# First four token chunks on different PSUM tiles, weight and activation loads on other queues, and the second tile's cast and transposes one step earlier

## The chip, the cores and the metric

The kernel runs on one core of one Trainium2 chip. A core has four compute engines that run side by side, each with its own queue of instructions: TensorE (PE in the profile, its weight loads PEld), VectorE (DVE), ScalarE (ACT) and GpSimd (POOL). SyncE (SP) issues data transfers (DMAs). An engine takes its instructions in the order in which they were written, and an instruction that waits holds back everything behind it on that engine. The metric is the device time of one execution in microseconds (us), smaller is better.

## What is computed

The input x has 8 sequences of 4096 tokens with 192 channels. A causal convolution of 7 taps mixes each token with the six before it; the 24 channels of each of 8 heads share one set of tap weights, a softmax over 7 numbers. The result goes through a two-layer network with 2048 hidden units and the activation h * sigmoid(beta * h). Cut to what matters:

```python
w = softmax(weight, axis=-1)                         # 8 heads x 7 taps
out = np.einsum('hk,bskhg->bshg', w, x_unf)          # x_unf: the 7 last tokens of each token
h = out.reshape(32768, 192) @ w_in                   # 192 -> 2048
g = h * (1.0 / (1.0 + np.exp(-beta * h)))
return (g @ w_out).astype(np.float32)                # 2048 -> 192
```

## The kernel before

**Tiling.** The 32768 tokens are two streams of 16384 (s = 0 and 1) that are worked side by side, each on 64 of the 128 partitions; the 192 channels are three groups (kk) of 64. A *tile* j is 512 tokens of both streams. The work goes in *steps* (lines 65 to 69): steps 0 and 1 take 128 tokens of each stream, step 2 takes 256, steps 3 to 8 take 256 each, and all later ones take 512. In step i the kernel runs the first matmul (mm1) of step i, with the activation on ScalarE right behind it, and between its units the second matmul (mm2) of step i-1. A step has 16 units of 128 hidden columns; steps 0 to 2 take them in pairs (`mm1_pair`, u = 0 to 7: hidden columns u and u + 8, one on each half of the partitions, so that only half of w_in is needed on each), later steps one by one (`mm1`, u = 0 to 15).

**The order of the work** is written out by hand: `pin` keeps every instruction in program order on its engine. Waits between engines are derived from the tiles that instructions read and write.

**Start (lines 116 to 252).** The tap weights, the first chunk of x and beta are loaded by SP and ACT. GpSimd builds the two masks `sel` and `ident` and then issues its loads: four pieces of w_in, chunks 1 to 3 of x (`load_x0`, 128 tokens of both streams each), four pieces of w_out, four pieces of the second tile of x (`load_x(1, ...)`), then four copies of w_in from one half of the partitions to the other, and at last the casts of blocks 2 and 3 of the second tile. The softmax of the taps is left unnormalised in `etap`; its sum's reciprocal `rsum` is applied on the way out of PSUM. Seven diagonal matrices `diag[k]` hold the taps. `warm` issues matmuls on zeros, whose result nobody reads.

**The first tile (chunks b = 0 to 3)** is convolved on TensorE: `transpose_0` (three transposes into PSUM), `take_0` (copy to `xr`), `halo_0` (last six columns to the next chunk), `conv_0` (14 matmuls with `diag`), `evac_0` (scaled copy to `xc_of`, one for each stream). Chunk 0 is done before step 0, chunks 1 to 3 between the units of step 0 and after u = 0 of step 1. `scale_w_out` (VectorE, 16 pieces) divides w_out by beta between them.

**PSUM** is two pools of two tiles, each of two banks: `psum_h` (name ph) and `psum_o` (name po). A tile that is asked for waits until the one that had the buffer two requests earlier is no longer in use. Before the change one `misc` tile of psum_h holds the output of `warm`, the taps and beta, and `cv0`, the other psum_h tile, holds both streams of chunk 0's convolution.

**From the second tile on** (step 3 and later) the convolution is VectorE's: `cast_x` (float32 to bfloat16), `transpose_x` (DMA transpose on SP, one per block of 128 tokens) into `xt`, then `conv_ops`: tap 0 on line 279, taps 1 to 6 on line 281, the last one writing `xc`, which mm1 reads. `load_x` fetches tiles two ahead on SP. These operations stand in the list `work`, and `vector_work` writes them out between the units of mm1: each call adds to a budget (1300 in step 2, 653 in steps 3 to 8), and operations are written while the budget is above zero, each costing its planned ns (929 for a 256-token tap, 850 for a cast). Since DVE runs in program order, this decides also how much work stands ahead of `store` (line 356), the copy of a finished mm2 result out of psum_o.

**Step 2, u = 0, before the change** casts blocks 0 and 1 of the second tile, issues its four transposes and the loads of tile 3; at the end of step 1 the loads of tile 2 have been issued. `vector_work` begins at u = 1.

Of the kernel before, what the change touches and what calls it, by code (L numbers as in the profile page):

```python
# [10 lines left out]
FP32 = mybir.dt.float32  # L11
# [8 lines left out]
def kernel(  # L20
# [60 lines left out]
    def cast_x(j, s, b0=0, b1=NB, eng=None):  # L81
        if j not in xbf_of:
            xbf_of[j] = xbf_pool.tile([128, NB, NK, NS, Q], BF16, name="xb")
        pin((eng or nc.vector).tensor_copy(  # L84
            xbf_of[j][:, b0:b1, :, s, :].rearrange("p b k q -> p k b q"),
            xf_of[j][:, b0:b1, s, :].rearrange("p b (q k) -> p k b q", k=NK)))
# [4 lines left out]
    def transpose_x(j, b):  # L91
        if j not in xt_of:
            new_xt(j)
        c = LEAD + 128 * b
        pin(nc.sync.dma_start_transpose(  # L95
            out=xt_of[j][:, :, c:c + 128],
            in_=xbf_of[j][:, b, :, :, :].rearrange("p k s q -> p (k s q)")))
# [30 lines left out]
    scrap = consts.tile([128, 1], FP32, name="scrap")  # L128
    pin(nc.scalar.activation(scrap, one, AF.Exp))


    sel = consts.tile([H, NS, H, Q // H], FP32, name="sel")
    pin(nc.gpsimd.memset(sel, 0.0))
# [3 lines left out]
    pin(nc.gpsimd.memset(ident, 0.0))  # L137
    pin(nc.gpsimd.affine_select(out=ident, in_=ident, compare_op=ALU.not_equal, fill=1.0,
                                base=0, pattern=[[-1, 128]], channel_multiplier=1))
    HF = F // 2  # L140

    def load_x0(b):
        pin(nc.gpsimd.dma_start(out=x0[:, b, :, :],
                                in_=xs[:, 128 * b:128 * b + 128, :].rearrange("s p d -> p s d")))

    for f in range(0, HF, 512):
        for s in range(NS):
            load_w_in(s, HF * s + f, HF * s + f + 512)
        if f == 0:
            load_x0(1)  # L150
    load_x0(2)
    for c in range(0, NF, 4):
        pin(nc.gpsimd.dma_start(out=w_out_f[:, c:c + 4, :], in_=w_out_v[:, c:c + 4, :]))
        if c == 0:
            load_x0(3)
    for b in (0, 2):
        for s in range(NS):
            load_x(1, s, b, b + 2, nc.gpsimd)
# [3 lines left out]
    for s in range(NS):  # L162
# [5 lines left out]
    ident2 = consts.tile([128, NS, Q], FP32, name="ident2")  # L168
    pin(nc.vector.tensor_tensor(out=ident2, in0=ident[:, None, 0:Q].to_broadcast([128, NS, Q]),
                                in1=ident[:, None, Q:].to_broadcast([128, NS, Q]), op=ALU.add))  # L170
    misc = psum_h.tile([128, 2, TILE], FP32, name="ph")

    def warm(n, cols):
        for _ in range(n):
            pin(nc.tensor.matmul(misc[:, 0, 0:cols], zeros[:, 0:128], zeros[:, 0:cols], start=True, stop=True))  # L175

    warm(9, 256)
    tap_ps = misc[:, 1, 0:K]
    pin(nc.tensor.matmul(tap_ps, sel.rearrange("h s g j -> h (s g j)"), taps, start=True, stop=True))
    nmax = consts.tile([128, 1], FP32, name="nmax")  # L180
    pin(nc.vector.tensor_reduce(out=nmax, in_=tap_ps, axis=AX.X, op=ALU.max, negate=True))
# [1 line left out]
    tsum = consts.tile([128, 1], FP32, name="tsum")  # L183
    pin(nc.scalar.activation(etap, tap_ps, AF.Exp, bias=nmax, accum_out=tsum))
    diag = consts.tile([128, K, NS, Q], FP32R, name="diag")
    for k in range(K):
        pin(nc.vector.tensor_scalar_mul(diag[:, k, :, :], ident2, etap[:, k:k + 1]))
    rsum = consts.tile([128, 1], FP32, name="rsum")
    pin(nc.vector.reciprocal(rsum, tsum))


    place = [(0, 0), (1, 0), (2, 0), (2, 128)]
# [21 lines left out]
    def conv_0(cv, b, k0=0, k1=K):  # L214
        for k in range(k0, k1):
            for s in range(NS):
                pin(nc.tensor.matmul(  # L217
                    cv[:, s, 0:NK * 128], diag[half_of(s), k, :, :].rearrange("p s q -> p (s q)"),
                    xr[b][half_of(s), :, k:k + 128], start=(k == 0), stop=(k == K - 1)))

    def evac_0(cv, b, s, eng):
        i, c = place[b]
        src = cv[:, s, 0:NK * 128].rearrange("p (k t) -> p k t", k=NK)
        dst = xc_of[i][:, s, :, c:c + 128]
        if eng is nc.scalar:
            pin(nc.scalar.activation(dst, src, AF.Copy, scale=rsum))
        else:
            pin(eng.tensor_scalar_mul(dst, src, rsum))  # L228

    def po_tile():  # L230
        return psum_o.tile([128, 2, TILE], FP32, name="po")

    new_xt(0)
    po01 = po_tile()
    t0_ = transpose_0(po01[:, 0, :], 0)
    take_0(t0_, 0, act=True)
    beta_ps = misc[:, 1, 16:16 + NF]
    pin(nc.tensor.transpose(beta_ps, beta16, ident[0:NF, 0:NF]))
    beta = consts.tile([128, NF], FP32, name="beta")
    pin(nc.vector.tensor_copy(beta, beta_ps))  # L240
    warm(3, 128)
    pin(nc.scalar.activation(scrap, one, AF.Silu))
    cv0 = psum_h.tile([128, 2, TILE], FP32, name="ph")
    conv_0(cv0, 0)
    evac_0(cv0, 0, 0, nc.scalar)
    evac_0(cv0, 0, 1, nc.vector)
    warm(6, 128)
    rbeta = consts.tile([128, NF], FP32, name="rbeta")
    pin(nc.vector.reciprocal(rbeta, beta))
    tapn = consts.tile([128, K], FP32, name="tapn")  # L250
# [89 lines left out]
    def mm2(i, pr, phase, fc):  # L340
        if phase == 0 and fc == 0:
            po_of[pr] = psum_o.tile([128, 2, TILE], FP32, name="po")
        po = po_of[pr]
        for half in range(2):
            q = half ^ phase
            s, b = pr[q]
            r = half_of(half)
            pin(nc.tensor.matmul(po[:, q, 0:D], g_of[i][r, fc, s, ts(b, 128)], w_out_s[r, fc, :],  # L348
                                 start=(phase == 0 and fc == 0), stop=(phase == 1 and fc == NF - 1)))
        if phase == 1 and fc == NF - 1:  # L350
            store(i, pr, po)
# [56 lines left out]
    for i in range(n_steps):  # L408
        plan = mm2_plan(i - 1) if i else [[] for _ in range(NF)]
        g_of[i] = g_pool.tile([128, NF, NS, TILE], BF16, name="g")  # L410
        if i == 0:
            for u in range(NF // 2):
                mm1_pair(0, u)
                if u == 0:
                    t = transpose_0(po01[:, 1, :], 1)
                    take_0(t, 1)
                    halo_0(t, 1)
                elif u == 1:
                    cv = po_tile()
                    conv_0(cv, 1)  # L420
                    for s in range(NS):
                        evac_0(cv, 1, s, nc.vector)
                elif u == 2:
                    po23 = po_tile()
                    t = transpose_0(po23[:, 0, :], 2)
                    take_0(t, 2)
                    halo_0(t, 2)
                elif u == 4:
                    cv = po_tile()
                    conv_0(cv, 2)  # L430
                    for s in range(NS):
                        evac_0(cv, 2, s, nc.vector)
                elif u == 6:
                    t = transpose_0(po23[:, 1, :], 3)
                    take_0(t, 3)
                    halo_0(t, 3)
                if u >= 4:
                    for c in range(2 * (u - 4), 2 * (u - 3)):
                        scale_w_out(c)
            continue  # L440
        if i < NP:
            for u in range(NF // 2):
                mm1_pair(i, u)
                if i == 1 and u == 0:
                    for c in range(8, 12):
                        scale_w_out(c)
                    cv = po_tile()
                    conv_0(cv, 3)
                    for c in range(12, NF):
                        scale_w_out(c)  # L450
                    for s in range(NS):
                        evac_0(cv, 3, s, nc.vector)
                for t in plan[2 * u] + plan[2 * u + 1]:
                    mm2(i - 1, *t)
                if i == 2:
                    if u == 0:
                        for s in range(NS):
                            cast_x(1, s, 0, 2)
                        for b in range(NB):
                            transpose_x(1, b)  # L460
                        for s in range(NS):
                            load_x(3, s)
                    else:
                        vector_work(i, 1300, flush=u == NF // 2 - 1)
            if i == 1:
                for s in range(NS):
                    load_x(2, s)
            continue
        for u in range(NF):
            mm1(i, u)  # L470
            for t in plan[u]:
# [34 lines left out]
```

## Time and profile before

| | |
|---|---|
| median of 3 runs | 703.62 us (702.87 to 704.54) |
| the profiled execution: its own time / its span from first to last instruction | 704.65 us / 702.9 us |
| TensorE busy (matmuls / weight loads) | 689.8 / 542.6 us |
| VectorE, ScalarE, GpSimd busy | 541.4, 587.4, 15.9 us |
| PE busy in 0 to 50 us | 39.9 of 50 us |
| PE busy in 50 to 690 us | 640 of 640 us |
| DMA, share of 16 engines' time, 11 to 18 us | 1.01 to 1.08 |

The row of PE in 0 to 50 us is the sum of five stretches of 10 us (7.45, 9.43, 8.74, 7.40, 6.91). Between 50 and 690 us the matmuls follow each other without a gap. The profile counts a matmul as busy over its whole length though neighbours overlap, so a busy PE is not a measure of throughput. Numbers such as L348 are lines of the kernel; x16 behind a row means 16 instructions merged.

### The profile page before, as it was taken

What the parts mean: (1) busy time and instruction counts of PE and PEld (TensorE: products, weight loads), DVE (VectorE), ACT (ScalarE), POOL (GpSimd) and SP (SyncE); (2) the same over time, 40 slices, a digit from 0 to 9 for tenths busy, and PEclk for the clock granted to TensorE, in tenths of its full rate; (3) what the DMA queues carried; (4) which work ended last, traced back from release to release, by engine and by line L of the source; (5) the groups of instructions that cost most, each with busy time, mean ns of one, the idle gap of its engine ahead of it and who ended that gap; (6) DMA issues with size and microseconds to landing.
All of it is one profiled execution on the core that took longest, in us unless ns stands there. A gap on an engine that the chain in (4) does not pass through costs nothing.

```text
span 702.9 us, 25421 instructions
## 1 busy us (share of the span) xinstructions
PE 689.8 (98%) x11561; PEld 542.6 (77%) x11561; DVE 541.4 (77%) x901; ACT 587.4 (84%) x600; POOL 15.9 (2%) x29
## 2 busy tenths in 40 slices
PE   8879999999999999999999999999999999999998
PEld 5669997777777777777777777777777777777777
DVE  3499999999988877877977787887787887785002
ACT  4869999888888888888888888888888888888882
POOL 7100000000000000000000000000000000000000
PEclk9999999999999999999999999999999999999999
DMA  8535333434433342334342333343333342111112
GB/s 207 132 92 159 103 104 92 117 109 109 112 103 101 105 114 64 89 104 100 104 114 77 80 101 97 104 114 80 82 97 103 97 114 70 48 47 47 33 40 69
DMA packets 120572, 67.33 MB, mean 96 GB/s; under 512 B 55024, under 2 KB 119616, under 8 KB 120464
## 3 DMA queue, kind: packets, MB, share of 16 engines
q1 hardware_dynamic: 118336, 61.08, 31.6%
q0 software_dynamic: 1984, 4.52, 2.8%
q8 instruction: 90, 1.47, 0.9%
q14 instruction: 18, 0.15, 0.1%
q10 hardware_dynamic: 144, 0.10, 0.1%
HBM read 28.32 MB, written 25.17 MB: 76 GB/s over the span
## 4 chain that ended last, share of the span: by engine, by line
PE 94%; DMA 2%; DVE 2%; POOL 1%; SPq 0%; issue 0%; ACT 0%; POOLq 0%; DVEq 0%
PE po L348 46%; PE ph L311 46%; PE po L371 2%; DMA w_in_s<-in_moe_w_in_dram 1%; DMA xf<-in_x_dram 1%; DVE acc L281 1%; DMA xt<-xb 0%; PE ph L298 0%; POOL w_in_s L110 0%; PE po L217 0%; POOL xf L78 0%; DVE w_out_s L255 0%; SPq L95 0%; DVE xc L281 0%; SPq L78 0%
## 5 line engine op out<-in xcount | busy, mean ns | idle before, releaser
L314 ACT ACTIVATE g<-ph,beta 128x1024 bf16<-128x1024 f32 (+1 forms) x544 | 561.0, 1039 | 89.7 <-PE ph L311 86.0
L348 PEld LDWEIGHTS <-g 64*128 64x128 bf16 x7936 | 362.3, 94 | 92.8 <-issue 0.2
L348 PE MATMUL po<-w_out_s,g 64*128 64x192 bf16 x7936 | 427.9, 243 | 0.0
L311 PE MATMUL ph<-xc,w_in_s 64*128 64x512 bf16 (+1 forms) x3264 | 420.3, 358 | 5.0 <-DVE xc L281 5.0
L281 DVE SCALAR_TENSOR_TENSOR acc<-xt,tapn,acc 128x512 f32<-128x512 bf16 (+1 forms) x450 | 315.3, 763 | 0.9
L311 PEld LDWEIGHTS <-w_in_s 64*128 64x128 bf16 x3264 | 168.9, 94 | 51.6 <-issue 5.2
L356 DVE COPY o_sb<-po 128x384 f32<-128x384 f32 x124 | 69.0, 557 | 130.6 <-PE po L348 128.8
L281 DVE SCALAR_TENSOR_TENSOR xc<-xt,tapn,acc 128x512 bf16<-128x512 bf16 (+1 forms) x90 | 64.2, 763 | 0.2
L84 DVE CAST xb<-xf 128x768 bf16<-128x768 f32 (+1 forms) x62 | 48.9, 826 | 0.0
L279 DVE TENSOR_SCALAR acc<-xt,tapn 128x512 f32<-128x512 bf16 (+1 forms) x90 | 40.5, 501 | 6.5 <-DMA xt<-xb 5.4
L302 ACT ACTIVATE g<-ph,beta 128x256 bf16<-128x256 f32 (+1 forms) x48 | 22.0, 564 | 7.4 <-PE ph L298 6.9
L298 PE MATMUL ph<-xcp,w_in_s 64*128 64x256 bf16 (+1 forms) x144 | 15.2, 320 | 2.1 <-ACT g L302 1.4
L298 PEld LDWEIGHTS <-w_in_s 64*128 64x128 bf16 x144 | 7.2, 98 | 6.2 <-issue 4.2
L371 PE MATMUL po<-w_out_s,g 128*128 128x192 bf16 x128 | 10.7, 246 | 0.0
L371 PEld LDWEIGHTS <-g 128*128 128x128 bf16 x128 | 10.5, 98 | 0.2 <-issue 0.2
L374 DVE COPY o_sb<-po 128x192 f32<-128x192 f32 x8 | 2.9, 358 | 7.6 <-PE po L371 7.6
L228 DVE TENSOR_SCALAR xcp<-po,rsum 128x384 bf16<-128x384 f32 x6 | 3.4, 610 | 4.2 <-PE po L217 4.2
L217 PE MATMUL po<-xr,diag 64*128 64x384 f32 x42 | 5.7, 415 | 0.6 <-DVE xr L208 0.6
L175 PE MATMUL ph<-zeros 128*128 128x256 bf16 (+1 forms) x18 | 3.4, 362 | 2.4 <-DVE beta L240 1.3
L217 PEld LDWEIGHTS po<-xr,diag 64*128 64x128 f32 x42 | 4.5, 230 | 1.3 <-DVE xr L208 1.2
L175 PEld LDWEIGHTS <-zeros 128*128 128x128 bf16 x18 | 2.1, 137 | 3.3 <-issue 1.8
L270 DVE COPY xt<-xt 128x18 bf16<-128x18 bf16 x28 | 4.5, 160 | 0.0
(46 smaller groups left out, 42.9 us busy)
## 6 DMA issues: line engine op xcount, KB each, us to landing
out_dram<-o_sb SPq DMA_DIRECT2D x124, 192.0 KB, 2.7
xf<-in_x_dram SPq DMA_DIRECT2D x60, 384.0 KB, 4.2
xt<-xb SPq DMA_TRANSPOSE x124, 2.4
w_out_f<-in_moe_w_out_dram POOLq DMA_DIRECT2D x4, 384.0 KB, 7.5
w_in_s<-in_moe_w_in_dram POOLq DMA_DIRECT2D x4, 192.0 KB, 6.1
xf<-in_x_dram POOLq DMA_DIRECT2D x4, 192.0 KB, 7.3
w_in_s<-w_in_s POOLq DMA_DIRECT2D x4, 192.0 KB, 7.5
out_dram<-o_sb SPq DMA_DIRECT2D x8, 96.0 KB, 1.6
```

Source lines behind the costliest of these rows:

```text
L84: pin((eng or nc.vector).tensor_copy(xbf_of[j][:, b0:b1, :, s, :].rearrange("p b k q -> p k b q"), xf_of[j][:, b0:b1, s, :].rearrange("p b ...
L175: pin(nc.tensor.matmul(misc[:, 0, 0:cols], zeros[:, 0:128], zeros[:, 0:cols], start=True, stop=True))
L217: pin(nc.tensor.matmul(cv[:, s, 0:NK * 128], diag[half_of(s), k, :, :].rearrange("p s q -> p (s q)"), xr[b][half_of(s), :, k:k + 128], sta ...
L279: pin(nc.vector.tensor_scalar_mul(a, src, w))
L281: pin(nc.vector.scalar_tensor_tensor(out=xc_of[i][:, k0:k1, 0:n] if k == K - 1 else a, in0=src, scalar=w, in1=a, op0=ALU.mult, op1=ALU.add))
L298: pin(nc.tensor.matmul(ph[:, h, 0:NS * n], w_in_s[half_of(h), kk, ts(fcs[h], 128)], xc_of[i][half_of(h), :, kk, :], start=(kk == 0), stop= ...
L302: pin(nc.scalar.activation(g_of[i][:, fcs[h], :, 0:n], ph[:, h, 0:NS * n].rearrange("p (s t) -> p s t", s=NS), AF.Silu, scale=beta[:, fcs[ ...
L311: pin(nc.tensor.matmul(ph[:, s, 0:n], w_in_s[half_of(s), kk, ts(fc, 128)], xc_of[i][half_of(s), kk, 0:n], start=(kk == 0), stop=(kk == NK ...
L314: pin(nc.scalar.activation(g_of[i][:, fc, :, 0:n], ph[:, :, 0:n], AF.Silu, scale=beta[:, fc:fc + 1]))
L348: pin(nc.tensor.matmul(po[:, q, 0:D], g_of[i][r, fc, s, ts(b, 128)], w_out_s[r, fc, :], start=(phase == 0 and fc == 0), stop=(phase == 1 a ...
L356: pin(nc.vector.tensor_copy(o_sb, po[:, :, 0:D]))
L371: pin(nc.tensor.matmul(po[:, 0, 0:D], g_of[i][:, fc, s, ts(b, 128)], w_out_s[:, fc, :], start=(fc == 0), stop=(fc == NF - 1)))
```

## The change

It has four parts. (1) The load of the first piece of w_in is issued by GpSimd ahead of the masks, and chunks 1 to 3 of x are loaded by SP instead of GpSimd. (2) PSUM: `warm` writes a psum_h tile of its own, `idle`; the taps share `cv0` with stream 0 of chunk 0's convolution; beta and stream 1 of it go to a new psum_o tile, `po_b`. So ScalarE and VectorE read chunk 0's two results from different tiles, and psum_o has one request more ahead of all later ones. (3) Only two of the diagonal matrices are made before beta's copy, the other five and `rsum` after it; the warming matmuls are 8 and 5 instead of 9 and 6. (4) Blocks 0 and 1 of the second tile are cast and transposed after u = 4 of step 1 instead of u = 0 of step 2; blocks 2 and 3 are transposed at the end of step 1, behind the loads of tile 2, with the loads of tile 3 behind them. `vector_work` thereby begins at u = 0 of step 2.

```diff
+    load_w_in(0, 0, 512)
+
+    def load_x0(b, eng=nc.gpsimd):
+        pin(eng.dma_start(out=x0[:, b, :, :],
+                          in_=xs[:, 128 * b:128 * b + 128, :].rearrange("s p d -> p s d")))
+
+    for b in range(1, NB):
+        load_x0(b, nc.sync)
...
     for f in range(0, HF, 512):
         for s in range(NS):
-            load_w_in(s, HF * s + f, HF * s + f + 512)
-        if f == 0:
-            load_x0(1)
-    load_x0(2)
+            if f or s:
+                load_w_in(s, HF * s + f, HF * s + f + 512)
     for c in range(0, NF, 4):
         pin(nc.gpsimd.dma_start(out=w_out_f[:, c:c + 4, :], in_=w_out_v[:, c:c + 4, :]))
-        if c == 0:
-            load_x0(3)
...
-    misc = psum_h.tile([128, 2, TILE], FP32, name="ph")
+    idle = psum_h.tile([128, 2, TILE], FP32, name="ph")
...
-    warm(9, 256)
-    tap_ps = misc[:, 1, 0:K]
+    warm(8, 256)
+    cv0 = psum_h.tile([128, 2, TILE], FP32, name="ph")
+    tap_ps = cv0[:, 1, 0:K]
...
-    for k in range(K):
+    def make_diag(k):
         pin(nc.vector.tensor_scalar_mul(diag[:, k, :, :], ident2, etap[:, k:k + 1]))
-    rsum = consts.tile([128, 1], FP32, name="rsum")
-    pin(nc.vector.reciprocal(rsum, tsum))
+    for k in range(2):
+        make_diag(k)
...
-    beta_ps = misc[:, 1, 16:16 + NF]
+    po_b = po_tile()
+    beta_ps = po_b[:, 1, 0:NF]
     pin(nc.tensor.transpose(beta_ps, beta16, ident[0:NF, 0:NF]))
     beta = consts.tile([128, NF], FP32, name="beta")
     pin(nc.vector.tensor_copy(beta, beta_ps))
+    for k in range(2, K):
+        make_diag(k)
+    rsum = consts.tile([128, 1], FP32, name="rsum")
+    pin(nc.vector.reciprocal(rsum, tsum))
     warm(3, 128)
...
-    cv0 = psum_h.tile([128, 2, TILE], FP32, name="ph")
-    conv_0(cv0, 0)
-    evac_0(cv0, 0, 0, nc.scalar)
-    evac_0(cv0, 0, 1, nc.vector)
-    warm(6, 128)
+    b0 = [cv0[:, 0, :], po_b[:, 0, :]]
+    conv_0(b0, 0)
+    evac_0(b0, 0, 0, nc.scalar)
+    evac_0(b0, 0, 1, nc.vector)
+    warm(5, 128)
...
                 for t in plan[2 * u] + plan[2 * u + 1]:
                     mm2(i - 1, *t)
+                if i == 1 and u == 4:
+                    for s in range(NS):
+                        cast_x(1, s, 0, 2)
+                    for b in range(2):
+                        transpose_x(1, b)
                 if i == 2:
-                    if u == 0:
-                        for s in range(NS):
-                            cast_x(1, s, 0, 2)
-                        for b in range(NB):
-                            transpose_x(1, b)
-                        for s in range(NS):
-                            load_x(3, s)
-                    else:
-                        vector_work(i, 1300, flush=u == NF // 2 - 1)
+                    vector_work(i, 1300, flush=u == NF // 2 - 1)
             if i == 1:
                 for s in range(NS):
                     load_x(2, s)
+                for b in range(2, NB):
+                    transpose_x(1, b)
+                for s in range(NS):
+                    load_x(3, s)
```

More of the change, by code (lines that the diff above doesn't have):

```diff
@@ L129 @@
     pin(nc.scalar.activation(scrap, one, AF.Exp))
+    HF = F // 2
+    load_w_in(0, 0, 512)
[4 more added lines that the diff above has]
+        load_x0(b, nc.sync)
     sel = consts.tile([H, NS, H, Q // H], FP32, name="sel")
@@ L139 @@
                                 base=0, pattern=[[-1, 128]], channel_multiplier=1))
[L140 to L144, printed above, removed]
     for f in range(0, HF, 512):
         for s in range(NS):
-            load_w_in(s, HF * s + f, HF * s + f + 512)
-        if f == 0:
-            load_x0(1)
-    load_x0(2)
+            if f or s:
+                load_w_in(s, HF * s + f, HF * s + f + 512)
     for c in range(0, NF, 4):
         pin(nc.gpsimd.dma_start(out=w_out_f[:, c:c + 4, :], in_=w_out_v[:, c:c + 4, :]))
-        if c == 0:
-            load_x0(3)
     for b in (0, 2):
@@ L170, with po_tile @@
                                 in1=ident[:, None, Q:].to_broadcast([128, NS, Q]), op=ALU.add))
-    misc = psum_h.tile([128, 2, TILE], FP32, name="ph")
+    def po_tile():
+        return psum_o.tile([128, 2, TILE], FP32, name="po")
+    idle = psum_h.tile([128, 2, TILE], FP32, name="ph")
     def warm(n, cols):
         for _ in range(n):
-            pin(nc.tensor.matmul(misc[:, 0, 0:cols], zeros[:, 0:128], zeros[:, 0:cols], start=True, stop=True))
-    warm(9, 256)
-    tap_ps = misc[:, 1, 0:K]
+            pin(nc.tensor.matmul(idle[:, 0, 0:cols], zeros[:, 0:128], zeros[:, 0:cols], start=True, stop=True))
+    warm(8, 256)
+    cv0 = psum_h.tile([128, 2, TILE], FP32, name="ph")
+    tap_ps = cv0[:, 1, 0:K]
     pin(nc.tensor.matmul(tap_ps, sel.rearrange("h s g j -> h (s g j)"), taps, start=True, stop=True))
@@ L212, in halo_0, with conv_0 @@
         pin(nc.vector.tensor_copy(dst, t[:, :, 128 - PAD:]))
-    def conv_0(cv, b, k0=0, k1=K):
-        for k in range(k0, k1):
+    def conv_0(cv, b):
+        for k in range(K):
             for s in range(NS):
                 pin(nc.tensor.matmul(
-                    cv[:, s, 0:NK * 128], diag[half_of(s), k, :, :].rearrange("p s q -> p (s q)"),
+                    cv[s][:, 0:NK * 128], diag[half_of(s), k, :, :].rearrange("p s q -> p (s q)"),
                     xr[b][half_of(s), :, k:k + 128], start=(k == 0), stop=(k == K - 1)))
@@ L222, in evac_0 @@
         i, c = place[b]
-        src = cv[:, s, 0:NK * 128].rearrange("p (k t) -> p k t", k=NK)
+        src = cv[s][:, 0:NK * 128].rearrange("p (k t) -> p k t", k=NK)
         dst = xc_of[i][:, s, :, c:c + 128]
@@ L228, in evac_0, with banks @@
             pin(eng.tensor_scalar_mul(dst, src, rsum))
-    def po_tile():
-        return psum_o.tile([128, 2, TILE], FP32, name="po")
+    def banks(po):
+        return [po[:, 0, :], po[:, 1, :]]
     new_xt(0)
@@ L418 @@
                 elif u == 1:
-                    cv = po_tile()
+                    cv = banks(po_tile())
                     conv_0(cv, 1)
@@ L428 @@
                 elif u == 4:
-                    cv = po_tile()
+                    cv = banks(po_tile())
                     conv_0(cv, 2)
@@ L446 @@
                         scale_w_out(c)
-                    cv = po_tile()
+                    cv = banks(po_tile())
                     conv_0(cv, 3)
```

## The prediction

> **What bounds the kernel now.** I read the page first.
>
> ```profile
> PE 689.8 (98%) x11561; PEld 542.6 (77%) x11561; DVE 541.4 (77%) x901; ACT 587.4 (84%) x600; POOL 15.9 (2%) x29
> ...
> PE   8879999999999999999999999999999999999998
> ```
>
> TensorE is the bound, and only the first three slices (up to 53 us) and the last one show gaps. The change touches nothing after step 2, so its worth is what it takes from the start: how much earlier PE enters the stretch without gaps. The second view is the list of waits for 0 to 70 us (total, times, longest).
>
> ```profile
> ACT g L302 <- PE ph L298: 6.9, 6, 2.1
> DVE acc L279 <- DMA xt<-xb: 5.4, 1, 5.4
> PE ph L311 <- DVE xc L281: 5.0, 1, 5.0
> ...
> DVE xcp L228 <- ACT xcp L226: 3.8, 1, 3.8
> ...
> PE ph L175 <- DVE beta L240: 1.3, 1, 1.3
> ```
>
> The largest PE wait is one piece of 5.0 us, for VectorE's convolution of step 3 (xc), and VectorE itself waited 5.4 us for the transposed second tile. The timeline shows how they hang together.
>
> ```profile
> 24.62 1.13 DVE L228 TENSOR_SCALAR xcp<-po,rsum 128x384 bf16<-128x384 f32 x2
> ...
> 29.02 0.56 DVE L356 COPY o_sb<-po 128x384 f32<-128x384 f32 x1 [3.27 <-PE po L348]
> 29.49 0.90 DVE L84 CAST xb<-xf 128x384 bf16<-128x384 f32 x2
> 30.06 1.07 SPq L78 DMA_DIRECT2D xf<-in_x_dram  x2
> 31.18 5.18 SPq L95 DMA_TRANSPOSE xt<-xb  x4
> 35.86 0.75 DVE L279 TENSOR_SCALAR acc<-xt,tapn 128x768 f32<-128x768 bf16 x1 [5.40 <-DMA xt<-xb]
> 41.92 1.02 DVE L281 SCALAR_TENSOR_TENSOR xc<-xt,tapn,acc 128x768 bf16<-128x768 bf16 x1
> 43.09 0.82 PE L311 MATMUL ph<-xc,w_in_s 64*128 64x256 bf16 x6 [5.02 <-DVE xc L281]
> 46.61 0.50 PE L311 MATMUL ph<-xc,w_in_s 64*128 64x256 bf16 x6
> ```
>
> DVE is idle from 25.75 to 29.02, behind a store of step 0; then come the casts, two loads on SP ahead of the transposes, and the convolution, which ends at 42.94. PE had run out at 38.06 (last rows of step 2: start 37.47, 0.59). After the pause six matmuls take 0.82 us, later 0.50. Last, the first 11 us:
>
> ```profile
> 4.30 1.69 DVE L187 TENSOR_SCALAR diag<-ident,etap 128x128 fp32r<-128x128 f32 x7 [0.43 <-ACT etap L184]
> 4.45 0.28 PE L238 MATMUL ph<-ident,beta 16*128 16x16 f32 x1
> 6.08 0.48 PE L175 MATMUL ph<-zeros 128*128 128x128 bf16 x3 [1.35 <-DVE beta L240]
> 6.49 2.61 PE L217 MATMUL ph<-xr,diag 64*128 64x384 f32 x14
> 9.14 0.58 ACT L226 ACTIVATE xcp<-ph,rsum 128x384 bf16<-128x384 f32 x1 [2.58 <-PE ph L217]
> 9.75 0.62 DVE L228 TENSOR_SCALAR xcp<-ph,rsum 128x384 bf16<-128x384 f32 x1 [3.76 <-ACT xcp L226]
> 10.52 0.82 PE L298 MATMUL ph<-xcp,w_in_s 64*128 64x256 bf16 x6 [0.67 <-DVE xcp L228]
> ```
>
> PE waits 1.35 us for a copy of beta, and VectorE's half of the evacuation starts only when ScalarE's is over.
>
> **What the Trainium skill says.** "TensorE: Matmul & The Clock Gate", Part 1, says that PE runs at half clock until it has been busy for a window of about 3.4 us and falls back after an idle one. The trace agrees: granted clock 0.51 in 43.0 to 46.4 us and 1.00 after it, behind a pause of 5.0 us. "PSUM — Partial Sum Buffer", PSUM bank collisions, asks for a guard by bank where two engines meet. Here the guard is wider: the warming matmuls write bank 0 of `misc` and wait for a DVE read of bank 1, so two tiles should part the engines. "DMA: Bandwidth & Descriptors", Issuing engines are not separate DMA queues, says that another issuing engine saves issue time only, since all share the same 16 DMA engines; the DMA share of 1.01 to 1.08 in 11 to 18 us fits that.
>
> **The change, part by part.**
>
> *Diagonals, beta, PSUM tiles.* Beta's transpose ends at 4.73, as before (taps, x's first chunk and `ident` set it; `ident` moves from 1.92 to about 2.6, hidden, since its first PE user is at 3.60). The warming matmuls no longer wait: 4.73 + 0.48 = 5.2. The first convolution matmul needs xr (ACT, 4.55 + 0.49 = 5.04) and beta's copy (DVE after two diagonals of 0.24: 4.8 to 5.05). The other five diagonals follow each 0.24 us, faster than PE's pair of 2 x 2.61/14 = 0.37, so they stay ahead. Convolution 5.2 to 7.8, both evacuations side by side to 8.45, first mm1 at 8.55 against 10.52: 2.0 us. `rsum` (0.31) is done by 6.6. One warming matmul fewer costs or gains at most 0.23, hidden by the wait for the taps' load; I take nothing.
>
> *Loads.* GpSimd issues one w_in piece (0.69) ahead of masks that took 1.19 (0.73 to 1.92), so the second piece leaves at about 2.6 as now, where it landed 5.6 later, at 8.2. But SP's three x loads (0.4 us each, from 2.05 on, 192 KB each) now run beside it. Between no delay and the 590 KB at the 320 GB/s of the full stretch (1.8 us) it lands at 8.2 to 10.0. I take 8.9, so 0.4 of the 2.0 is lost. GpSimd is rid of three issues of 0.74 and of waits before its later ones; its queue drains some 3 us earlier, which only hidden loads feel. SP has nothing else to do there. The new request in psum_o makes the convolution of chunk 1 wait for `halo_0` (0.17 at 12.69) as well: 0.1.
>
> *Clock.* The matmuls of step 0 run at half speed until about 15.2 (convolution 2.61 then, 1.53 at 17.14), the gaps of 1.35 and 0.67 being two of its causes. With PE nearly closed from 1.05 to 8.5 it may speed up before mm1; the cold rows from 10.52 to 15.24 would shrink by up to 1.7, of which ScalarE's 0.85 per pair takes some back. Bounds 0 and 1.7; I take 0.5. The front is worth 1.6 - 0.1 + 0.5 = 2.0, and all of it reaches the end of step 2, because DVE and ACT behind it run nearly closed (ACT rows of 5.81 and 9.37 us).
>
> *Casts and transposes.* On the old clock: DVE is free at 25.75, casts 0.90 to 26.65; the pieces of x landed by 21.3. SP is idle then; first transpose's issue 1.29, the second starts at 27.94 and lands in 2.4 (as those at 45.4 to 49.2, in a quiet stretch) to 3.3 (as now): 30.3 to 31.3, against 35.78. Seven taps take 7.09 (35.86 to 42.95), so step 3's xc is ready at 37.4 to 38.4; I take 37.8. The store at 29.02 is in front of the taps and still over by 29.6. SP's later queue: store, tile 2 (still 30.06), blocks 2 and 3, tile 3; blocks 2 and 3 are needed only by step 4's taps, some 10 us later. PE ends step 2 at 38.06 and goes on at once: 5.0 us. It stays at full clock: the first four units of step 3 took 47.27 - 43.09 = 4.18 instead of 4 x 0.655 = 2.62 (the spacing of the later ones): 1.55 more.
>
> *What comes late next.* `vector_work` is called eight times in step 2 instead of seven, so 1300 planned ns, one or two taps of 1.05, stand ahead of every later store, and stores free PSUM for PE.
>
> ```profile
> 53.33 0.54 DVE L356 COPY o_sb<-po 128x384 f32<-128x384 f32 x1
> 64.08 0.55 DVE L356 COPY o_sb<-po 128x384 f32<-128x384 f32 x1
> ```
>
> Today the first ends at 53.88 and PE needs its buffer at 55.48; the second ends at 64.63, needed at 66.02. Counting the reordered DVE row by row from the end of step 3's convolution (E), the second ends at E + 22.6. PE, no longer cold, wants it at E + 0.3 + 2 x 10.53 + 0.33 = E + 21.7. So about 0.9 us comes back as short stalls in steps 4 to 6; as DVE's five convolutions to step 8 need 42.4 us and PE's four steps 42, it does not grow. Bounds 0 and 2.
>
> *Sum.* 2.0 + 5.0 + 1.55 - 0.9 = 7.65. The profiled execution, 704.65 (span 702.9 and 1.75 around it), becomes 697.0; it lay 1.03 above the median, so the median of 703.62 becomes 696.0.
>
> **The rivals.**
>
> A, as above: 696.0, with the bounds (front 1 to 3.5, return 0 to 2) 693.0 to 698.0. Chance 0.58.
>
> B, the front gives nothing: w_in's second piece lands at 10 or later behind SP's loads, or the two evacuations wait for each other through their common xc tile. For: DMA is busy 0.7 to 1.27 of its time from 2 to 9 us. Against: w_in's first piece leaves 1.1 us earlier. The casts and transposes alone, 5.65: 698.0, range 697 to 699.5. Chance 0.19.
>
> C, VectorE becomes the bound from step 3 to 8: 98% busy in 50 to 80 us already, late stores cost 3 to 5 us. Against: its 42.4 us. 700.8, range 699.5 to 702. Chance 0.11.
>
> D, slower: the same late stores without recovery. If DVE's work per 256-token step exceeds PE's 10.5 us, each of two stores in six steps stalls PE by one tap (1.05): 12.6 us, less 7.65 plus the 0.9 already counted, gives 707.7. It decides from 10.5 us of DVE per step; now it is 8.5. Chance 0.07.
>
> E, the transposes gain nothing, as if step 3 waited for something not shown (x's second tile late); gains and returns cancel: 703. Chance 0.05.
>
> **How the numbers follow.** This measurement can tell 0.2% (1.4 us) from no change. A, B and C are faster: 0.88; E same 0.05; D slower 0.07. A, B and the lower part of C hold 0.8: 693.0 to 700.2.
>
> **What would show it.** The first L298 matmul near 8.5 to 9 and no DVE wait for ACT at L228; the last tap of step 3 at about 36 and PE's wait before the first L311 under 1 us, its six matmuls at 0.5 us; small PE waits on o_sb or DVE between 45 and 75 us. Wrong would be: a first L298 that waits for w_in, a PE wait of 3 us or more before L311, or PE stalls of over 2 us in steps 4 to 8.

## The result and the profile after

The changed kernel took 697.41 us (median of 4 runs, 697.36 to 698.42), beside 703.83 us for the kernel before (4 runs, 702.87 to 704.54): a ratio of 0.9913, interval 0.9896 to 0.993, so 6.4 us faster. Its profiled execution took 697.36 us with a span of 695.6, where the one of before took 704.65 with 702.9.

The page of the changed kernel, engine totals and the 40 slices:

```profile
PE 686.9 (99%) x11559; PEld 538.6 (77%) x11559; DVE 541.8 (78%) x901; ACT 587.2 (84%) x600; POOL 13.7 (2%) x26
...
PE   8999999999999999999999999999999999999998
```

The digits 8 and 7 in the second and third slice have become 9. The list of waits from 0 to 70 us (total, times, longest) says what is left:

```profile
DVE acc L291 <- DMA xt<-xb: 1.9, 1, 1.9
...
PE ph L323 <- DVE xc L293: 0.7, 1, 0.7
...
PE po L246 <- DMA beta<-in_moe_beta_dram: 0.6, 1, 0.6
PE po L360 <- DVE o_sb L368: 0.5, 1, 0.5
...
PE ph L310 <- DMA w_in_s<-in_moe_w_in_dram: 0.4, 1, 0.4
```

The wait of 5.0 us for step 3's convolution (now L323 for L293) is 0.7, and VectorE's wait of 5.4 us for the transposed tile is 1.9. Three new ones stand beside them: beta's load, w_in's load, and a store (`o_sb`) that frees PSUM too late. The timeline of the changed kernel, 22 to 50 us (the last two rows from the views of VectorE and of PE alone), answers to the one shown of before:

```profile
23.16 0.88 DVE L84 CAST xb<-xf 128x384 bf16<-128x384 f32 x2
...
24.07 3.52 SPq L95 DMA_TRANSPOSE xt<-xb  x2
...
26.27 0.56 DVE L368 COPY o_sb<-po 128x384 f32<-128x384 f32 x1 [2.23 <-PE po L360]
...
28.79 0.75 DVE L291 TENSOR_SCALAR acc<-xt,tapn 128x768 f32<-128x768 bf16 x1 [1.88 <-DMA xt<-xb]
...
34.85 1.02 DVE L293 SCALAR_TENSOR_TENSOR xc<-xt,tapn,acc 128x768 bf16<-128x768 bf16 x1
...
36.01 0.50 PE L323 MATMUL ph<-xc,w_in_s 64*128 64x256 bf16 x6 [0.71 <-DVE xc L293]
...
46.99 0.54 DVE L368 COPY o_sb<-po 128x384 f32<-128x384 f32 x1
...
47.59 0.51 PE L360 MATMUL po<-w_out_s,g 64*128 64x192 bf16 x8 [0.53 <-DVE o_sb L368]
```

The casts now stand ahead of the store of step 0 (26.27) instead of behind it, the first tap starts at 28.79 instead of 35.86, step 3 at 36.01 instead of 43.09, and its first six matmuls take 0.50 us, no longer 0.82. At 47.59 the late store shows. The front, in the same view:

```profile
4.89 0.28 PE L246 MATMUL po<-ident,beta 16*128 16x16 f32 x1 [0.59 <-DMA beta<-in_moe_beta_dram]
...
5.54 0.69 PE L224 MATMUL ph<-xr,diag 64*128 64x384 f32 x1
...
8.18 0.58 ACT L233 ACTIVATE xcp<-ph,rsum 128x384 bf16<-128x384 f32 x1 [1.84 <-PE po L224]
8.22 0.62 DVE L235 TENSOR_SCALAR xcp<-po,rsum 128x384 bf16<-128x384 f32 x1 [1.43 <-PE po L224]
...
8.98 0.32 PE L310 MATMUL ph<-xcp,w_in_s 64*128 64x256 bf16 x1 [0.19 <-DVE xcp L235]
9.68 0.50 PE L310 MATMUL ph<-xcp,w_in_s 64*128 64x256 bf16 x5 [0.38 <-DMA w_in_s<-in_moe_w_in_dram]
...
11.37 1.53 PE L224 MATMUL po<-xr,diag 64*128 64x384 f32 x14 [0.22 <-DVE xr L214]
```

ScalarE and VectorE now take the two results side by side. Yet PE first waits for beta's load and then, after one of the six matmuls, for w_in's second piece. The six are complete from 9.68 on, against 10.52 before: 0.84 us of the 2.0 hoped for from the PSUM tiles.

### The profile page after: what moved, and what is told of

Read it like the earlier page. It is cut to its first block, busy times and chain, and to the rows that moved or that the text cites. A ratio compares the mean times of both kernels' runs of the same rounds, so it can differ in the third digit from the quotient of the medians.

```text
span 695.6 us, 25420 instructions
## 1 busy us (share of the span) xinstructions
PE 686.9 (99%) x11559; PEld 538.6 (77%) x11559; DVE 541.8 (78%) x901; ACT 587.2 (84%) x600; POOL 13.7 (2%) x26
## 4 chain that ended last, share of the span: by engine, by line
PE 92%; DVE 5%; DMA 1%; issue 1%; SPq 0%; POOL 0%; DVEq 0%; POOLq 0%
PE po L360 45%; PE ph L323 45%; DVE acc L293 3%; PE po L383 2%; DMA w_in_s<-in_moe_w_in_dram 1%; DVE w_out_s L267 1%; DVE xb L84 1%; PE po L224 0%; DVE acc L291 0%; DMA xt<-xb 0%; SPq L95 0%; DVE o_sb L368 0%; PE ph L310 0%; DVE xcp L235 0%; PE po L206 0%
## 5 line engine op out<-in xcount | busy, mean ns | idle before, releaser
L323 PE MATMUL ph<-xc,w_in_s 64*128 64x512 bf16 (+1 forms) x3264 | 419.0, 357 | 0.7 <-DVE xc L293 0.7
L293 DVE SCALAR_TENSOR_TENSOR acc<-xt,tapn,acc 128x512 f32<-128x512 bf16 (+1 forms) x450 | 315.4, 764 | 0.9
L323 PEld LDWEIGHTS <-w_in_s 64*128 64x128 bf16 x3264 | 167.7, 94 | 47.5 <-PE po L360 0.9
L293 DVE SCALAR_TENSOR_TENSOR xc<-xt,tapn,acc 128x512 bf16<-128x512 bf16 (+1 forms) x90 | 64.2, 765 | 0.2
L383 PEld LDWEIGHTS <-g 128*128 128x128 bf16 x128 | 10.5, 98 | 0.2 <-issue 0.2
L224 PE MATMUL po<-xr,diag 64*128 64x384 f32 x49 | 7.1, 379 | 0.3 <-DVE xr L214 0.2
L267 DVE TENSOR_SCALAR w_out_s<-w_out_f,rbeta 128x192 bf16<-128x192 f32 x16 | 4.5, 353 | 0.0
```

Of the source, the lines that this page charges most:

```text
L224: pin(nc.tensor.matmul(cv[s][:, 0:NK * 128], diag[half_of(s), k, :, :].rearrange("p s q -> p (s q)"), xr[b][half_of(s), :, k:k + 128], sta ...
L267: pin(nc.vector.tensor_scalar_mul(w_out_s[:, c, :], w_out_f[:, c, :], rbeta[:, c:c + 1]))
L293: pin(nc.vector.scalar_tensor_tensor(out=xc_of[i][:, k0:k1, 0:n] if k == K - 1 else a, in0=src, scalar=w, in1=a, op0=ALU.mult, op1=ALU.add))
L323: pin(nc.tensor.matmul(ph[:, s, 0:n], w_in_s[half_of(s), kk, ts(fc, 128)], xc_of[i][half_of(s), kk, 0:n], start=(kk == 0), stop=(kk == NK ...
L383: pin(nc.tensor.matmul(po[:, 0, 0:D], g_of[i][:, fc, s, ts(b, 128)], w_out_s[:, fc, :], start=(fc == 0), stop=(fc == NF - 1)))
```

## The experiments

To place a gain, one *mark* is used in every trace: the start of the `o_sb` copy that follows step 8, 105.46 us before and 97.82 after. From it to the last copy to `o_sb` every one of these traces takes 594.5 us, within 0.03; what comes after that last copy takes 2.9 to 3.3 us, so a span can move by up to 0.4 us more or less than its mark. All profiles are single executions; "first mm1" is the start of the row of matmuls that no longer stops.

| kernel | beta's load lands after | first mm1 | 14 convolution matmuls of chunk 1 | start of step 3 | mark | span | median us; ratio to before (interval) |
|---|---|---|---|---|---|---|---|
| before | 1.7 | 10.52 | 2.61 | 43.09 | 105.46 | 702.9 | 703.83 |
| changed | 3.2 | 9.68 | 1.53 | 36.01 | 97.82 | 695.6 | 697.41; 0.9913 (0.9896 to 0.993) |
| e8, the same again | 4.0 | 9.76 | 1.50 | 36.66 | 98.50 | 696.2 | 698.01; 0.9914 (0.99 to 0.9929) |
| e1, part 4 alone | 1.7 | 10.52 | 2.57 | 38.25 | 100.06 | 697.5 | 698.19; 0.9912 (0.9882 to 0.9942) |
| e11, e1 again | 1.8 | 10.51 | 1.52 | 37.21 | 99.02 | 696.4 | 698.73; 0.9932 (0.9907 to 0.9957) |
| e2, parts 1 to 3 alone | 4.1 | 9.82 | 1.51 | 40.98 | 103.82 | 701.6 | 703.85; 0.9988 (0.9972 to 1.0005) |
| e3, x on GpSimd | 3.2 | 8.96 | 2.61 | 37.33 | 99.14 | 696.5 | one run, 698.32 |
| e4, seven calls | 4.2 | 9.95 | 1.51 | 36.58 | 97.78 | 695.5 | one run, 697.32 |
| e5, one PSUM tile | 3.8 | 10.18 | 2.48 | 38.12 | 99.92 | 697.6 | one run, 699.42 |
| e6, casts on GpSimd | 4.1 | 9.84 | 1.52 | 38.16 | 99.48 | 697.2 | 698.61; 0.9923 (0.9903 to 0.9943) |
| e7, e6 with e9's edits | 2.6 | 9.38 | 1.51 | 35.87 | 97.19 | 694.9 | 696.69; 0.9902 (0.9885 to 0.9918) |
| e9, loads and calls | 2.2 | 9.26 | 1.51 | 34.76 | 95.96 | 693.7 | 696.16; 0.9896 (0.9872 to 0.992) |
| e10, beta on ScalarE | 2.0 | 9.85 | 2.11 | 37.14 | 98.93 | 696.6 | 698.98; 0.993 (0.9907 to 0.9953) |

Each of e1 to e11 was measured beside the kernel before, whose medians in the three groups of runs were 704.44, 703.91 and 702.82; so medians of different groups are compared by their ratios.

### The parts apart: e1, e2, and both kernels again

The theory: part 4 (casts and transposes a step earlier) carries most of the gain, and the front little. e1 is the kernel before with part 4 alone, e2 the changed kernel with part 4 undone. e1's edit, in part:

```diff
                 for t in plan[2 * u] + plan[2 * u + 1]:
                     mm2(i - 1, *t)
+                if i == 1 and u == 4:
+                    for s in range(NS):
+                        cast_x(1, s, 0, 2)
+                    for b in range(2):
+                        transpose_x(1, b)
                 if i == 2:
...
+                    vector_work(i, 1300, flush=u == NF // 2 - 1)
...
```

> The kernel before, with part 4 alone (casts and transposes of the second tile after u = 4 of step 1, vector_work from u = 0 of step 2). The theory of the prediction: 5.0 us of PE's wait go, 1.55 of the cold start go, 0.9 come back as late stores, so about 5.6 us faster than before (698.0). Rival, that the front is needed too (the second tile lands too late for the early cast, or the late stores eat it): under 3 us faster. In the trace: first mm1 of step 0 still at 10.5, last tap of step 3 ready at 37.4 to 38.4, PE's wait ahead of step 3 under 0.7.

> The changed kernel with part 4 undone, so parts 1 to 3 alone. The trace of the changed kernel ends step 2's matmuls at 35.3 instead of 38.06, so the theory expects about 2.7 us faster than before (701.0), with a PE wait of about 5 us ahead of step 3 and the cold start behind it both still there. Rival: the earlier end of step 2 is only a longer wait for step 3's convolution, whose transposes start when they did, and less than 1 us is left.

e1's mark is 5.40 us before that of the kernel before, and its span 5.4 shorter. Its convolution ends at 38.10, PE's wait ahead of step 3 is gone, and the matmuls behind it run at full speed, as expected:

```profile
10.52 0.82 PE L298 MATMUL ph<-xcp,w_in_s 64*128 64x256 bf16 x6 [0.67 <-DVE xcp L228]
...
12.83 2.57 PE L217 MATMUL po<-xr,diag 64*128 64x384 f32 x14
15.25 0.50 PE L298 MATMUL ph<-xcp,w_in_s 64*128 64x256 bf16 x6
...
38.25 0.50 PE L311 MATMUL ph<-xc,w_in_s 64*128 64x256 bf16 x6
```

e2 keeps the old pause; its timeline from 30 to 45 us:

```profile
33.76 0.75 DVE L291 TENSOR_SCALAR acc<-xt,tapn 128x768 f32<-128x768 bf16 x1 [5.62 <-DMA xt<-xb]
...
40.98 0.82 PE L323 MATMUL ph<-xc,w_in_s 64*128 64x256 bf16 x6 [5.25 <-DVE xc L293]
```

All of it is 2.1 us earlier than before, the pause as long (5.25 us, six matmuls at 0.82). At the mark 1.64 remain, and in the timed runs nothing that can be told from zero: 0.9988, interval 0.9972 to 1.0005, which is 0.8 us with bounds of -0.4 and 2.0. The 2.7 us expected of e2 didn't come; its rival, under 1 us, fits the timed runs.

In e2 and in the changed kernel chunk 1's convolution ran fast (1.51, 1.53), in before and e1 it didn't (2.61, 2.57). The granted clock of these traces can't say why: it reads 1.00 from 5 to 16 us in all of them. But six matmuls of mm1 take 0.82 or 0.50 us here, the same two lengths as behind the pause at 43 us, where granted clocks of 0.51 and 1.00 are on record. So "clock down" and "clock up" in the front are read from such lengths. Is the early clock the front's doing? e8 is the changed kernel and e11 is e1, neither with any edit.

> The changed kernel itself, beside the others on one chip, for the size of the change: the trace of its first run shows 7.3 us less span, its median 6.4 less. The theory keeps 7.3 give or take 0.8; where beta lands moves it by up to 0.9 from run to run.

> e1 once more (the kernel before with part 4 alone), with more rounds and beside the others, since its first times spread over 3.4 us. Its trace had 5.4 us less span than before: 698.4 to 698.7 in time, ratio 0.992 to 0.993, so 1.0 to 2.0 us above the changed kernel. Rival: the front is worth nothing in time and e1 is level with the changed kernel, 697.4 to 698.0.

The same rows of e11 show that the old front can have it too:

```profile
10.51 0.50 PE L298 MATMUL ph<-xcp,w_in_s 64*128 64x256 bf16 x6 [0.67 <-DVE xcp L228]
...
12.21 1.52 PE L217 MATMUL po<-xr,diag 64*128 64x384 f32 x14 [0.22 <-DVE xr L208]
```

The same kernel, the same start at 10.5, the same wait of 0.67 ahead of it; but here the clock was up, and the mark lies 1.04 us earlier (99.02 for 100.06). So the moment at which PE's clock comes up differs between executions of one kernel. The Trainium skill, "TensorE: Matmul & The Clock Gate", Part 1, says that the window which decides it runs freely and that the transition varies by about 500 ns either way. That it varies agrees; the size doesn't: rows are slow until about 15.2 in e1 and fast from 10.51 on in e11, over 4 us apart, and the measurement decides. Whether the new front makes an early clock likelier isn't shown: the row of chunk 1 took about 1.5 us in 7 of 10 profiles with it or a variant of it, and in 1 of 3 with the old one.

With the clock up in both, the front is worth 0.5 to 1.2 us at the mark (e8 and the changed kernel, 98.50 and 97.82, against e11's 99.02) and 0.2 to 0.8 by the span; these are differences of single traces. By time it isn't separated from nothing: e1 is level with the change (0.9912), e11 0.0018 to 0.0019 above it, about 1.3 us, with intervals that overlap. e8's timed gain, 5.9 us, is under the 6.5 to 8.1 expected; its span gives 6.7.

### What the front waits for: e3, e5, e10

In e3 GpSimd issues chunks 1 to 3 of x again, in their old places among its other loads; in e5 both streams of chunk 0 go to the two banks of one tile; in e10 beta is loaded by ScalarE's queue.

```diff
 e3
-    for b in range(1, NB):
-        load_x0(b, nc.sync)
...
 e5
-    b0 = [cv0[:, 0, :], po_b[:, 0, :]]
+    b0 = [cv0[:, 0, :], cv0[:, 1, :]]
 e10
-    pin(nc.sync.dma_start(out=beta16, in_=moe_beta.rearrange("(c p) -> c p", p=128)))
+    pin(nc.scalar.dma_start(out=beta16, in_=moe_beta.rearrange("(c p) -> c p", p=128)))
```

> The changed kernel with the three loads of x's chunks 1 to 3 back on GpSimd at their old places between the weights. If SP's loads delay the second piece of w_in (landing 9.64) and beta (landing about 4.8), both land earlier here: beta by about 4.4, w_in's second piece by about 8.8, and the first mm1 starts near 8.6 to 9.0 instead of stopping at 9.68. If only GpSimd's own issue times count, w_in's second piece lands at 9.6 still. x's chunk 1 then comes later (about 10.5), and the transposes of chunk 1 can wait for it. Whole time within 0.7 us of the changed kernel either way.

> The changed kernel with both streams of chunk 0's convolution in one psum_h tile again (cv0), all else as changed. If the wait follows the tile, VectorE's evacuation starts only when ScalarE's has ended, 0.6 us after the convolution's end instead of with it, though the two read different banks. If it follows the common output tile xc, it was never gone by the split and the two are side by side here as well. For the time the theory now expects little: in the changed kernel the first mm1 stopped for w_in's second piece until 9.68, and 8.84 + 0.62 is 9.46; so the first mm1 ends its wait at 9.7 if beta lands as early as there (4.85), and the span is within 0.3 of 695.6; only where beta is late is the whole 0.6 lost.

> The changed kernel with beta's load on ACT's queue instead of SP's, nothing else. Beta landed between 4.8 and 5.8 in the runs of the changed kernel's front; here it should land by 4.0 and the convolution of chunk 0 start at about 5.2. If w_in's second piece (9.4 to 9.7) is what the first mm1 waits for, that start is worth at most 0.1 to 0.3 at the first mm1 and the span stays within 0.4 of the changed kernel's 695.6 to 696.2. If beta is the bound, the first mm1 starts near 8.7 and the span falls by 0.8.

**e3.** Without SP's loads of x beside it, w_in's second piece, issued at 3.15, landed after 6.0 us instead of 6.5 and stops the first mm1 by no more than the 0.2 us that its row is longer than 0.82:

```profile
8.96 1.02 PE L312 MATMUL ph<-xcp,w_in_s 64*128 64x256 bf16 x6 [0.19 <-DVE xcp L237]
```

That is 0.72 us before the changed kernel, so SP's loads of x do delay that piece. Beta still took 3.2 us and landed at about 4.8, not at the 4.4 expected: its delay doesn't need these loads. The execution had the clock down (six matmuls 1.02, convolution 2.61), which hides at its mark what the earlier start is worth; how it would end with the clock up stays open. Against e1, whose clock was down as well, its mark is 0.92 us earlier.

**e5.** The timeline of e5:

```profile
8.80 0.58 ACT L233 ACTIVATE xcp<-ph,rsum 128x384 bf16<-128x384 f32 x1 [2.46 <-PE ph L224]
9.42 0.62 DVE L235 TENSOR_SCALAR xcp<-ph,rsum 128x384 bf16<-128x384 f32 x1 [2.01 <-ACT xcp L233]
10.18 0.82 PE L310 MATMUL ph<-xcp,w_in_s 64*128 64x256 bf16 x6 [0.77 <-DVE xcp L235]
```

VectorE starts when ScalarE is over, 0.62 us behind it, although the banks are different and though in both kernels both write one xc tile. With two PSUM tiles the starts are 0.04 apart. So the wait, one of those that are derived from the tiles, follows the PSUM tile, and the rival that the common xc tile keeps it falls. In the changed kernel that gain is mostly hidden: 8.84, the end of its evacuation, and 0.62 more is 9.46, still ahead of w_in at about 9.65. That is arithmetic; no run shows it with beta's load equal.

**e10.** Beta lands after 2.0 us, ahead of its use, and the convolution starts at 4.89 instead of 5.54. But the timeline goes on:

```profile
4.89 0.68 PE L224 MATMUL ph<-xr,diag 64*128 64x384 f32 x1
...
8.33 0.37 PE L310 MATMUL ph<-xcp,w_in_s 64*128 64x256 bf16 x1 [0.18 <-DVE xcp L235]
9.85 0.82 PE L310 MATMUL ph<-xcp,w_in_s 64*128 64x256 bf16 x5 [1.16 <-DMA w_in_s<-in_moe_w_in_dram]
```

All that was won is lost in the stop for w_in's second piece, and the time (0.993) is no better than the change. With beta this early the front is bound by that load. In e2, e4, e6 and e8, where beta took 4.0 us or more, the first mm1 starts at 9.76 to 9.95 without a stop for w_in: there beta is the bound.

### The late stores: e4

`vector_work` is called seven times in step 2, as before, so that one tap fewer stands ahead of the later stores:

```diff
-                if i == 2:
+                if i == 2 and u:
                     vector_work(i, 1300, flush=u == NF // 2 - 1)
```

> The changed kernel with vector_work from u = 1 of step 2, as before the change, so one or two taps fewer stand ahead of each later store. The theory: the PE stalls of 0.53 at 47.6 and 0.30 at 58.7 vanish, 0.8 us faster in the span. Rival: VectorE sets the pace from step 3 on in any order, and the stalls only move to the first mm1 of a later step: same span within 0.2.

PE's waits in e4, 8 to 100 us, with no row for `o_sb`:

```profile
PE ph L310 <- ACT g L314: 1.4, 4, 0.5
PE ph L323 <- DVE xc L293: 0.6, 1, 0.6
PE ph L310 <- DVE xcp L235: 0.2, 1, 0.2
```

In the changed kernel PE lost 0.53 us at 47.59 and 0.30 at 58.74 (a spacing of 0.96 between two units of mm1 instead of 0.655), 0.83 together. e4 entered step 3 at 36.58, 0.57 later than the changed kernel because beta came later, and was level with it at the mark, 97.78 for 97.82: 0.61 us won, not all of the 0.83. The span alone (695.5 for 695.6) would have said that the stores cost nothing.

The other traces show the same price. With eight calls the mark lies 61.95 to 61.96 us behind the end of step 3's last tap on VectorE in the changed kernel, in e1 and in e11 (35.87, 38.10, 37.07), though the waits for `o_sb` that are listed for PE are 0.53, none and 0.22; with seven calls it is 61.34 in e4 and 61.35 in e9. So with eight calls VectorE seems to set the pace of this stretch, at a price of about 0.6 us, and an earlier front counts only as far as it ends that convolution earlier.

### A better version: e6, e7, e9

e6 lets GpSimd cast the whole second tile, so that its four transposes can go at once. e9 takes e4's and e10's edits and issues both first pieces of w_in ahead of the masks; e7 is e6 with all of e9's edits.

```diff
 e6 and e7
-    for s in range(NS):
-        cast_x(1, s, 2, 4, nc.gpsimd)
+    for b in (0, 2):
+        for s in range(NS):
+            cast_x(1, s, b, b + 2, nc.gpsimd)
...
                 if i == 1 and u == 4:
-                    for s in range(NS):
-                        cast_x(1, s, 0, 2)
-                    for b in range(2):
+                    for b in range(NB):
                         transpose_x(1, b)
...
 e7 and e9
-    load_w_in(0, 0, 512)
+    for s in range(NS):
+        load_w_in(s, HF * s, HF * s + 512)
...
```

> The changed kernel with the casts of blocks 0 and 1 of the second tile on GpSimd too, and all four transposes issued by SP at u = 4 of step 1. The theory: GpSimd casts at about 17.5 to 20.5, so the transposed tile is there by 24 and step 3's convolution starts right behind the store at 26.3 instead of at 28.8; it ends at about 34.1, step 2's matmuls at 35.3, so PE's wait of 0.71 ahead of step 3 goes, and VectorE is 1.2 us ahead, so the late stores stop PE no more: 1.2 to 1.5 us off the span, 694.2. Rival: VectorE is the pace from step 3 on in any case, or the transposes run into the loads of GpSimd and land no earlier: within 0.3 of the changed kernel.

> e6 with three more edits: beta loaded by ACT's queue right behind its half of x's first chunk, the first two pieces of w_in ahead of the masks, vector_work from u = 1 of step 2. Beta's load took 1.7 us in the kernel before and 3.2 to 4.2 in the runs whose first w_in piece leaves ahead of the masks; issued 0.5 us earlier it should land by 4.0. The second piece lands about 1 us earlier (8.6), the masks end 0.65 later (3.85) and hold the transposes and the convolution to about 5.7. First mm1 at about 9.0 without a stop: 0.5 to 0.7 less than e6, span about 693.5. Rival: the later masks give back what the earlier weights bring, span as e6.

> The changed kernel with beta on ACT's queue, the first two pieces of w_in ahead of the masks and vector_work from u = 1 of step 2, but the casts on VectorE as changed (e7 without the GpSimd casts). In e6 and e7 four scalings of w_out took 2.10 and 1.73 us against 1.00 while GpSimd cast; here they should take 1.0 again. Theory: first mm1 at 9.4 as in e7, step 3's convolution ends near 35.5, no late store stops PE: span 694.4, at or under e7's 694.9. Rival: the later end of the convolution (GpSimd's casts gave 1 us there) outweighs it, and a wait ahead of step 3 of 1 us or more is back: 695.5 or more.

**e6** brought nothing over the change: 0.9923; what was expected of it didn't come. Its timeline shows what was in the way:

```profile
17.70 2.10 DVE L268 TENSOR_SCALAR w_out_s<-w_out_f,rbeta 128x192 bf16<-128x192 f32 x4
...
17.84 0.71 POOL L84 CAST xb<-xf 128x384 bf16<-128x384 f32 x1
...
20.32 2.21 PE L225 MATMUL po<-xr,diag 64*128 64x384 f32 x14 [1.22 <-DVE xr L215]
...
23.23 0.84 ACT L315 ACTIVATE g<-ph,beta 128x256 bf16<-128x256 f32 x2 [3.23 <-PE ph L311]
```

Four scalings of w_out on VectorE take 2.10 us beside GpSimd's casts; in the changed kernel they take 1.00 (17.22 to 18.22). Chunk 3 is copied later, PE waits 1.22 for it and ScalarE 3.23. Part of this is the clock: behind that wait the granted clock was 0.50 from 21 to 24 us, so that chunk 3's convolution took 2.21 us for 1.50 in the changed kernel. The other three executions of e6 had a mean clock of 1.000 and took 698.07 to 699.37 us, e8's in the same group 697.59 to 698.11; so without that drop e6 brings nothing either. The Trainium skill, "SBUF — State Buffer", Who interferes with whom, says that VectorE and GpSimd have a common port that one of them locks; these numbers agree: one scaling took 0.98 us instead of 0.31 beside a cast of 0.71. Moving a cast to an idle engine thus made the busy one slower in the very stage that had to end early.

**e9** has the earliest step 3 of all:

```profile
9.26 0.50 PE L311 MATMUL ph<-xcp,w_in_s 64*128 64x256 bf16 x5 [0.19 <-DMA w_in_s<-in_moe_w_in_dram]
...
16.77 1.00 DVE L268 TENSOR_SCALAR w_out_s<-w_out_f,rbeta 128x192 bf16<-128x192 f32 x4
...
33.59 1.02 DVE L294 SCALAR_TENSOR_TENSOR xc<-xt,tapn,acc 128x768 bf16<-128x768 bf16 x1
34.76 0.50 PE L324 MATMUL ph<-xc,w_in_s 64*128 64x256 bf16 x6
```

The four scalings take 1.00 us again, the convolution is over at 34.61, and no wait stands ahead of the first matmul. The span, 693.7, is 9.2 under that of before and 1.9 under the change. Timed, its ratio of 0.9896 is the best of all, but its interval (0.9872 to 0.992) holds the change's 0.9913: in the trace it is ahead, by the time it isn't separated. e7 ends between the two in its trace (mark 97.19), its scalings at 1.73 us for four; the stop for w_in (0.37) that it was to lose is still there.

## Why the prediction was right, and which term was not

Forecast A was right in kind and, 1.4 us aside, in size: 696.0 was given, 697.41 came, within its range of 693.0 to 698.0. Its steps in turn:

**Casts and transposes, 5.0 and 1.55.** Right. The transposes were to land at 30.3 to 31.3 on the old clock; less the 2.0 counted for the front that is 28.3 to 29.3, and the first tap, which waits for them, starts at 28.79; in e1, on the old clock, it starts at 31.02. The last tap was put at about 36 and ends at 35.87. PE's wait is 0.71 (under 1 was said), the cold start is gone. Part 4 alone, with stores coming late, was to be worth 5.0 + 1.55 - 0.9 = 5.65; e1 has 5.4 by span and mark.

**Late stores, 0.9 back.** Right in kind, somewhat less in size: two stalls of 0.83 us together in the changed kernel, in the steps named and not growing afterwards; with seven calls the `o_sb` row is gone, and 0.6 us is won at the mark.

**The front, 2.0.** This is the step that was too large, in three terms. *Diagonals, beta, PSUM tiles* put the convolution at 5.2 with "Beta's transpose ends at 4.73, as before"; beta landed 3.2 us after its issue instead of 1.7 and the convolution started at 5.54; in e8, with 4.0 for beta, its transpose alone began at 5.67. *Loads* let w_in's second piece leave "at about 2.6 as now" and land at 8.9, for a loss of 0.4. It left at 3.14, since GpSimd's first load began only at 1.26 and the masks behind it at 2.00, and landed 6.5 us later instead of 5.6, at about 9.65. The first mm1 was complete from 9.68 on instead of 8.55, so with beta 1.13 of the 1.97 were lost. A first mm1 that waits for w_in was one of the prediction's own signs of being wrong, and rival B's mechanism; it came, with 0.38 us. *Clock* counted 0.5 as won by closing gaps; e1 and e11 differ by 1.04 us without any edit, so no run shows that the change wins it. The front's 2.0 is therefore 0.5 to 1.2 at the mark at equal clock, and 0.8 (-0.4 to 2.0) by e2's timed runs. No run undoes the order of the diagonals or the number of warming matmuls alone.

**The sum, 7.65.** The mark moved by 7.64 us and the profiled time by 7.29, so in the traces the sum is almost exact; but this is luck in part. The profile of before had the clock down in step 0 and the profile of the changed kernel had it up; by e1 and e11 that is worth about 1.0 of the 7.64, which leaves 6.6, near the timed gains of 6.4 and, in e8, 5.9. The prediction took the whole 7.65 from the *median*, though the profiled execution lay 1.03 above it. That the late clock is also what made that execution slower than the median is likely, but not shown.

**The rivals.** 697.41 lies in B's range (697 to 699.5) as well as in A's. That the front gives something is seen in the traces (9.68 for 10.52, and the marks above); by time B isn't excluded. C and D fell in size: no PE stall of over 0.6 us stands behind the start of step 3 in the changed kernel, though C's mechanism, VectorE as the bound, is there with about 0.6 us. E fell with e1: the second tile of x wasn't late. Not settled is why the loads land late, beyond what is said next.

## What to carry to other kernels

When one engine is busy 98% of the span, look for the longest single pause, ask which chain fills it, and start that chain in an earlier stage in which its engine is idle; that alone made most of this gain. Work on a front that ends in a load is worth only as much as the load comes earlier: winning 0.65 us ahead of w_in's piece gave a stop of 1.16 in place of one of 0.38. Before a microsecond of front is believed, the same kernel should be profiled twice, and rows of the same operation compared for their clock.

## What was not expected of the hardware

A load of 8 KB (beta) took 1.7 us before, and 3.2 to 4.2 in all kernels in which w_in's first piece left ahead of it, with SP's loads of x (changed, e2, e4 to e6, e8) or without them (e3); issued from ScalarE's queue at 1.15, ahead of w_in at 1.25, it took 2.0 to 2.6 (e7, e9, e10). W_in's own first piece left 0.6 us earlier (1.26 for 1.87) and landed later (6.86 for 6.07); in e3, without SP's loads of x beside it, it landed at 5.56. Issuing its second piece 1.1 us earlier (e7, e9) brought it 0.3 to 0.4 earlier. GpSimd's first DMA starts only at 1.26, after 0.81 us of waiting in its own queue. Beside the other early loads an earlier issue bought a fraction of itself at most.

In the profiled execution of e6 the granted clock fell to 0.50 for over 3 us behind a wait of only 1.22 us, less than the idle window of about 3.4 us of which the prediction speaks; in e11 it stayed at 1.00 behind a wait of 1.09. So a short wait can cost the clock too, though not in every execution.
